# Last 128 output rows projected by column halves, and batch 1's second half of head pairs moved up, in a fused attention and feed-forward kernel

## Chip, cores and metric

The kernel runs on one core of a Trainium2 chip. The metric is the device time of one execution in microseconds, as the median over several executions. All times below come from the profiled execution or from those runs.

## The reference

For each of 8 batches and 8 heads, with 576 tokens of width 64, attention without a softmax is computed, normalised and scaled per head; the heads are then joined to rows of width 512, and a feed-forward layer of width 2048 follows.

```python
kv  = einsum('bhsd,bhse->bhde', k, v)
o   = einsum('bhsd,bhde->bhse', q, kv)
rms = sqrt(mean(o * o, axis=-1, keepdims=True) + 1e-06)
x   = (o / rms * g_norm).transpose(0, 2, 1, 3).reshape(4608, 512)
h   = x @ w_in                                # 4608 x 2048
out = (h / (1 + exp(-1.702 * h))) @ w_out     # 4608 x 512, float32
```

## The kernel before

The 4608 rows are cut into nine tiles of 512 rows. Tiles 0 to 7 each hold 512 of the 576 tokens of one batch. The remaining 64 tokens of each of the eight batches together make tile 8, called t == B in the code; its input is x_rem.

The function dense works on one tile in two phases. In the first phase TensorE makes 16 blocks of the hidden layer, four accumulating matmuls each (hidden, line 439), and ScalarE applies the gate to each block (line 448) and writes gT. In the second phase the function project (lines 478 to 506) multiplies gT by w_out: for each of four row blocks mo of 128 rows, 16 matmuls of 512 columns (fo, line 482) accumulate into one PSUM bank. The bank is copied to osb in SBUF, and DMAs store the rows. For tiles 0 to 7 one copy by VectorE (or by ScalarE for odd mo in tile 0, which is called deep) moves the whole bank. For tile 8 VectorE copies columns 0 to 255 (line 492), then ScalarE columns 256 to 511 (line 493), and two DMAs, one on SyncE's queue (SP) and one on ScalarE's, each store 64 rows of 512 columns (line 506).

The attention of tile t + 1 is woven into tile t by hand. The two dictionaries units1 and units2 hold small steps: a step under key n of units2 is issued right after the n-th projection matmul. Every engine executes its own instructions strictly in the order in which they are written, so this order decides what waits behind what. In tile 0 the projection is interleaved: 16 groups of four matmuls, going round mo = 0, 1, 2, 3 four times. The bank of mo = 0 is therefore complete after step 51, that of mo = 1 after step 55, that of mo = 2 after step 59 and that of mo = 3 after step 63.

During tile 0's second phase, batch 1 is prepared by the class Second, for four head pairs c = 0 to 3:

- pack_k(c) (line 95) is a VectorE copy that rearranges keys from kraw into kbuf.
- kv(c) (line 408) is six matmuls on kbuf and vbuf. After an odd c, keep_kv (line 228) copies the two products on VectorE into kvb, as two instructions.
- out(c) (line 247) is one 512-column matmul that needs kvb, and then a Square on ScalarE (line 267).
- ss(c) is a matmul that sums the squares (line 325), and then Ln (line 327) and Exp (line 333) on ScalarE.
- apply(c) (line 339) is one VectorE instruction that multiplies the attention output by the scale and writes xT, the input of tile 1.

The steps of pairs 0 and 1 and of pairs 2 and 3 are placed in this way before the change: pack_k after steps 21, 21, 36, 36; kv after 23, 24, 43, 44; out after 27, 33, 47, 52; ss and apply seven steps after each out.

PSUM has eight banks in three pools: ps_a with three (tag "att": attention products), ps_h with three (hidden blocks, the banks of mo = 0 and 1 in tile 0, and batch 1's sums of squares) and ps_o with two (projection outputs, among them mo = 2 and 3 in tile 0). A new tile in a pool waits until the earlier user of its bank is done.

Tile 1 begins with four hidden blocks worked side by side (group = 4, called hG), in the order of ko and then of block. Blocks 0 to 2 take banks of ps_h, and the fourth takes one of ps_o (line 452). From block 4 on, the hidden blocks (hT) take a ps_h bank each in turn.

Of the kernel before, what the change touches and what calls it, by code (L numbers as in the profile page):

```python
# [8 lines left out]
F32 = mybir.dt.float32  # L9
# [3 lines left out]
P = 128  # L13
# [3 lines left out]
def kernel(  # L17
# [10 lines left out]
    nc = tc.nc  # L28

    B, H, S, D = q.shape  # L30
    DM = H * D
    DFF = moe_w_in.shape[1]
    NPAIR = H // 2
    FO = DFF // P
    KO = DM // P
    EPS = 1e-6
    SM = 512
    J = SM // P
    R = S - SM
    assert R == 64 and B * R == SM and KO == NPAIR and 2 * D == P  # L40
    NT = B + 1
    EARLY = 2
    PE_ = 96
    NJ = S // PE_
# [8 lines left out]
    ps_a = ctx.enter_context(tc.tile_pool(name="ps_a", bufs=3, space=bass.MemoryType.PSUM))  # L53
    ps_h = ctx.enter_context(tc.tile_pool(name="ps_h", bufs=3, space=bass.MemoryType.PSUM))
    ps_o = ctx.enter_context(tc.tile_pool(name="ps_o", bufs=2, space=bass.MemoryType.PSUM))
# [22 lines left out]
    w_out_sb = const.tile([P, FO, DM], F16)  # L78
# [66 lines left out]
    for n, queue in (("k", nc.sync), ("q", nc.scalar), ("v", nc.sync)):  # L145
# [3 lines left out]
            out=first[n].rearrange("p (h x) -> p h x", h=2), in_=early_src(n, 0, 0, 1)  # L149
# [7 lines left out]
        out=ident,  # L157
        in_=ident,
# [35 lines left out]
    class Attention:  # L194
        ss_pool = (ps_a, "att")

        def __init__(self, b):
            self.b, self.kb = b, kvb[b % 2]
            self.qT, self.o = {}, {}
            x = xpool.tile([P, KO * SM], F16, name="xT", tag="xT")  # L200
            if b < EARLY:
                self.x = xT[b] = x.rearrange("p (c n) -> p c n", c=KO)
# [231 lines left out]
    def dense(t, units1, units2, group, deep):  # L434
        x = xT.pop(t) if t < B else x_rem
        gT = gpool.tile([P, FO, SM], F16, name="gT", tag="gT")

        def hidden(h, fo, ko):
            nc.tensor.matmul(  # L439
                h,  # L440
                w_in_sb[:, ko, fo * P : (fo + 1) * P],
                x[:, ko],
                start=(ko == 0),
                stop=(ko == KO - 1),
            )

        def gate(h, fo):
            nc.scalar.activation(gT[:, fo, :], h, AFT.Gelu_apprx_sigmoid)  # L448

        hs = []  # L450
        for i in range(group):
            pool, tag = (ps_h, "hT") if i < 3 else (ps_o, "o") if i < 5 else (ps_a, "att")
            hs.append(pool.tile([P, SM], F32, name="hG", tag=tag))
        if group:
            if t == 0:
                order = [(ko, fo) for f in (0, 2) for ko in (0, 1) for fo in (f, f + 1)]
                order += [(2, fo) for fo in range(4)]
                order += [(ko, fo) for ko in (0, 1, 2) for fo in (4, 5)]
                order += [(KO - 1, fo) for fo in range(group)]
            else:  # L460
                order = [(ko, fo) for ko in range(KO) for fo in range(group)]
            for ko, fo in order:
                hidden(hs[fo], fo, ko)
            for fo in range(group):
                gate(hs[fo], fo)
        for fo in range(FO):
            if fo >= group:
                h = ps_h.tile([P, SM], F32, name="hT", tag="hT")
                for ko in range(KO):
                    hidden(h, fo, ko)  # L470
                gate(h, fo)
            for u in units1.get(fo, ()):
                u()

        osb = opool.tile([P, 4, DM], F32, name="osb", tag="osb")
        os = {}

        def project(mo, fo):
            if fo == 0:
                pool, tag = (ps_h, "hT") if deep and mo < 2 else (ps_o, "o")  # L480
                os[mo] = pool.tile([P, DM], F32, name="o", tag=tag)
            nc.tensor.matmul(  # L482
                os[mo],
                gT[:, fo, mo * P : (mo + 1) * P],
                w_out_sb[:, fo, :],
                start=(fo == 0),
                stop=(fo == FO - 1),
            )
            if fo == FO - 1:
                if t == B:  # L490
                    half = DM // 2
                    nc.vector.tensor_copy(osb[:, mo, 0:half], os[mo][:, 0:half])  # L492
                    nc.scalar.copy(osb[:, mo, half:DM], os[mo][:, half:DM])
                else:
                    copy = nc.scalar.copy if deep and mo % 2 else nc.vector.tensor_copy
                    copy(osb[:, mo, :], os[mo])  # L496
                if t == B:
                    for g in range(2):
                        rows = out[(2 * mo + g) * S : (2 * mo + g + 1) * S, :]
                        if 2 * mo + g < EARLY:  # L500
                            p0 = SM % PE_
                            rows = rows[bass.DynSlice(NJ * p0 + SM // PE_, R, step=NJ), :]
                        else:
                            rows = rows[SM:S, :]
                        queue = (nc.sync, nc.scalar)[g]
                        queue.dma_start(out=rows, in_=osb[g * R : (g + 1) * R, mo, :])

        if deep:
            steps = [(mo, 4 * i + k) for i in range(4) for mo in range(4) for k in range(4)]
        else:  # L510
            steps = [(mo, fo) for mo in range(4) for fo in range(FO)]
        for n, (mo, fo) in enumerate(steps):
            project(mo, fo)
            for u in units2.get(n, ()):
                u()
        if t < EARLY:

            n = 0
            while n < SM:
                mo, j, p = n // P, n // PE_, n % PE_  # L520
                m = min((mo + 1) * P, (j + 1) * PE_) - n
                nc.sync.dma_start(
                    out=out[t * S : (t + 1) * S, :][bass.DynSlice(NJ * p + j, m, step=NJ), :],
                    in_=osb[n % P : n % P + m, mo, :],
                )
                n += m
        elif t < B:
            nc.sync.dma_start(
                out=out[t * S : t * S + SM, :].rearrange("(p j) m -> p j m", j=J), in_=osb
            )  # L530
# [76 lines left out]

    for t in range(NT):
        b = t + 1
        u1, u2 = {}, {}  # L610

        def at1(i, f, *args):
            u1.setdefault(i, []).append(lambda: f(*args))

        def at2(i, f, *args):
            u2.setdefault(i, []).append(lambda: f(*args))

        def of(b, name, *args):
            return lambda: getattr(live[b], name)(*args)

        if t == 0:
            at1(7, of(0, "out", NPAIR))
            at2(4, setattr, a0, "ss_pool", Attention.ss_pool)
            at2(4, of(0, "ss", NPAIR, True))
            at2(4, of(0, "apply", NPAIR))
            at1(8, start, 1)
            at1(9, spread_g)
            for r in krem + vrem:
                at1(8, nc.vector.memset, r[R:P], 0.0)
            for c in range(NPAIR):  # L630
                at1(12, of(1, "pack_q", c))
                at2(9 + 3 * c, of(1, "q", c))
                at2((21, 21, 36, 36)[c], of(1, "pack_k", c))
                at2((23, 24, 43, 44)[c], of(1, "kv", c))
                o = (27, 33, 47, 52)[c]
                at2(o, of(1, "out", c))
                at2(o + 7, of(1, "ss", c))
                at2(o + 7, of(1, "apply", c))
            at2(14, load_batch, 2, vbuf[0:1, NPAIR - 1, 0:1])
        elif b < B:  # L640
            if t == 1:
                at2(46, setattr, live[1], "ss_pool", Attention.ss_pool)
                at2(46, of(1, "out", NPAIR))
                at2(53, of(1, "ss", NPAIR))
                at2(53, of(1, "apply", NPAIR))
            f0 = 7 if t == 1 else 2
            at1(f0, casts, b)
            at1(f0, start, b)
            at1(f0, of(b, "transpose_q"))
            if t + 2 < B:  # L650
                at1(f0, load_batch, t + 2)
            for c in range(NPAIR):
                at1((11 if t == 1 else 9) + c, of(b, "kv", c))
            at2(0, nc.scalar.preload_act_table_set, "natural_log_exp_and_others")
            for j in range(J):
                at2((1, 4, 8, 11)[j], of(b, "rows", j))
            at2(7, of(b, "turn", 0))
            at2(16, of(b, "turn", 2))
            at2(27, of(b, "out", NPAIR))
            at2(36, of(b, "ss", NPAIR))  # L660
            at2(36, of(b, "apply", NPAIR))
        dense(t, u1, u2, (6, 4)[t] if t < 2 else 0, t == 0)


# [28 lines left out]
```

## Time and profile before

| | us |
|---|---|
| median of 9 runs | 290.96 |
| lowest and highest run | 290.54, 291.59 |
| the profiled execution, its own time | 291.17 |
| span of the profiled execution | 289.4 |
| TensorE busy in the span | 280.6 |
| ScalarE busy | 151.1 |
| VectorE busy | 102.8 |
| GpSimd busy | 56.4 |

The span runs from the first to the last instruction in the trace; the execution's own time has 1.77 us around it. An engine's busy time is the union of the durations of its instructions. A matmul's listed duration includes its way through the array, so successive matmuls overlap in the list; what a matmul costs in a stream is the distance between two starts. The chain of waits goes back from the last instruction to whatever released each step. The word "issue" in it is time in which nothing that the trace shows was waited for.

### The profile page before, as it was taken

What the parts mean: (1) busy time and instruction counts of PE and PEld (TensorE: products, weight loads), DVE (VectorE), ACT (ScalarE), POOL (GpSimd) and SP (SyncE); (2) the same over time, 40 slices, a digit from 0 to 9 for tenths busy, and PEclk for the clock granted to TensorE, in tenths of its full rate; (3) what the DMA queues carried; (4) which work ended last, traced back from release to release, by engine and by line L of the source; (5) the groups of instructions that cost most, each with busy time, mean ns of one, the idle gap of its engine ahead of it and who ended that gap; (6) DMA issues with size and microseconds to landing.
All of it is one profiled execution on the core that took longest, in us unless ns stands there. A gap on an engine that the chain in (4) does not pass through costs nothing.

```text
span 289.4 us, 4052 instructions
## 1 busy us (share of the span) xinstructions
PE 280.6 (97%) x1598; PEld 134.8 (47%) x1598; DVE 102.8 (36%) x222; ACT 151.1 (52%) x263; POOL 56.4 (19%) x71
## 2 busy tenths in 40 slices
PE   7989999999999999999999999999999999999993
PEld 2434544455445544554455445544454444444441
DVE  2530434545461456037602760275218200110010
ACT  2667546856465644574457536653664364027310
POOL 8841000203500170008000710062005100000000
PEclk9999999999999999999999999999999999999998
DMA  8999999979989736892699658944601320020022
GB/s 175 198 207 205 204 176 349 215 179 352 194 192 323 168 73 188 259 269 54 181 200 333 69 163 218 338 72 127 138 0 23 86 111 0 0 112 35 0 73 73
DMA packets 67636, 45.79 MB, mean 158 GB/s; under 512 B 37666, under 2 KB 65314, under 8 KB 66850
## 3 DMA queue, kind: packets, MB, share of 16 engines
q1 hardware_dynamic: 58080, 37.43, 50.3%
q0 software_dynamic: 9008, 7.29, 16.0%
q10 hardware_dynamic: 530, 0.82, 1.0%
q8 instruction: 12, 0.20, 0.3%
q14 instruction: 6, 0.05, 0.1%
HBM read 36.70 MB, written 9.44 MB: 159 GB/s over the span
## 4 chain that ended last, share of the span: by engine, by line
PE 91%; DMA 3%; POOL 3%; ACT 1%; DVE 1%; issue 0%; POOLq 0%
PE o L482 42%; PE hT L439 40%; PE hG L439 3%; DMA w_in_sb<-in_moe_w_in_dram 3%; PE kvp L213 2%; PE outR L279 2%; POOL vbuf L88 1%; POOL qraw L88 1%; POOL kraw L88 1%; PE kvp L408 1%; PE kvp L221 0%; PE ss L325 0%; PE outT L247 0%; PE q L421 0%; PE outT L258 0%
## 5 line engine op out<-in xcount | busy, mean ns | idle before, releaser
L482 PE MATMUL o<-w_out_sb,gT 128*128 128x512 f16 x576 | 134.0, 379 | 0.0
L448 ACT ACTIVATE gT<-hT 128x512 f16<-128x512 f32 x134 | 80.0, 599 | 76.5 <-PE hT L439 76.5
L439 PE MATMUL hT<-xT,w_in_sb 128*128 128x512 f16 x472 | 107.4, 379 | 0.0
L439 PEld LDWEIGHTS <-w_in_sb 128*128 128x128 f16 x576 | 55.1, 98 | 63.5 <-issue 1.3
L482 PEld LDWEIGHTS <-gT 128*128 128x128 f16 x576 | 54.6, 98 | 57.9
L309 POOL TENSOR_TENSOR x<-xr,g_all 128x512 f16<-128x512 f32 x24 | 30.0, 1270 | 129.9 <-DVE xr L304 84.6
L496 DVE COPY osb<-o 128x512 f32<-128x512 f32 x30 | 20.6, 687 | 46.5 <-PE o L482 46.5
L290 DVE TENSOR_REDUCE sum<-sq 128x8 f32<-128x512 f16 x24 | 15.3, 678 | 23.9 <-ACT sq L287 23.9
L228 DVE CAST kvb<-kvp 64x256 f16<-64x256 f32 (+1 forms) x16 | 6.2, 389 | 43.1 <-PE kvp L221 42.0
L304 DVE TENSOR_TENSOR xr<-outR,sum 128x512 f32<-128x512 f32 x24 | 15.5, 686 | 4.9 <-ACT sum L301 4.0
L267 ACT ACTIVATE sq<-outT 128x512 f16<-128x512 f32 (+1 forms) x16 | 7.8, 488 | 13.0 <-PE outT L247 11.6
L327 ACT ACTIVATE ln<-ss,eps_t 128x512 f32<-128x512 f32 (+1 forms) x16 | 9.3, 580 | 9.6 <-PE ss L325 9.4
L439 PE MATMUL hT<-x_rem,w_in_sb 128*128 128x512 f16 x64 | 14.0, 379 | 0.0
L287 ACT ACTIVATE sq<-outR 128x512 f16<-128x512 f32 x24 | 12.9, 589 | 0.1
L300 ACT ACTIVATE sum<-sum,eps_t 128x16 f32<-128x16 f32 x12 | 3.7, 308 | 14.8 <-DVE sum L290 14.8
L136 DVE CAST qbuf<-qf 128x512 f16<-128x512 f32 x24 | 9.7, 468 | 3.6 <-DMA qf<-in_q_dram 3.6
L492 DVE COPY osb<-o 128x256 f32<-128x256 f32 x4 | 1.7, 425 | 25.7 <-PE o L482 25.7
L448 ACT ACT_TABLE_LOAD x8 | 10.3, 1283 | 0.1
L279 PEld LDWEIGHTS <-qTd 128*128 128x128 f16 x96 | 7.4, 98 | 5.7 <-issue 0.2
L213 PEld LDWEIGHTS <-kbuf 128*128 128x128 f16 x96 | 7.4, 98 | 5.7
L439 PE MATMUL hG<-xT,w_in_sb 128*128 128x512 f16 x40 | 9.3, 379 | 0.5 <-DMA w_in_sb<-in_moe_w_in_dram 0.5
L213 PE MATMUL kvp<-vbuf,kbuf 128*128 128x128 f16 x96 | 9.3, 219 | 0.0
(70 smaller groups left out, 150.6 us busy)
## 6 DMA issues: line engine op xcount, KB each, us to landing
kf<-in_k_dram SPq DMA_DIRECT2D x6, 1024.0 KB, 5.9
vf<-in_v_dram SPq DMA_DIRECT2D x6, 1024.0 KB, 8.4
qf<-in_q_dram SPq DMA_DIRECT2D x6, 1024.0 KB, 11.9
out_dram<-osb SPq DMA_DIRECT2D x6, 1024.0 KB, 4.2
w_out_sb<-in_moe_w_out_dram POOLq DMA_DIRECT2D x4, 512.0 KB, 17.2
out_dram<-osb SPq DMA_DIRECT2D x6, 192.0 KB, 2.6
out_dram<-osb SPq DMA_DIRECT2D x8, 128.0 KB, 2.4
w_in_sb<-in_moe_w_in_dram POOLq DMA_DIRECT2D x3, 256.0 KB, 8.0
```

The lines of the kernel that those rows point to most:

```text
L136: nc.vector.tensor_copy(out=dst[:, c, :, :].rearrange("p j (l d) -> p j l d", l=2), in_=src[n][:, h, :].rearrange("p l (j d) -> p j l d", ...
L213: nc.tensor.matmul(t[:, c, :].rearrange("p (l d) -> p l d", l=2), kh[:, c, j, :], vh[:, 2 * c : 2 * c + 2, j * D : (j + 1) * D], start=(j ...
L279: nc.tensor.matmul(t[:, c * P : (c + 1) * P], self.qT[c][:, j * P : (j + 1) * P], self.kb[:, c, :], start=True, stop=True,)
L287: nc.scalar.activation(sq, t, AFT.Square)
L290: nc.vector.tensor_reduce(out=self.sum2[:, j % 2, :], in_=sq.rearrange("p (h d) -> p h d", h=H), op=ALU.add, axis=mybir.AxisListType.X,)
L304: nc.vector.tensor_mul(xr, self.o[j + i].rearrange("p (h d) -> p h d", h=H), s2[:, i, :].unsqueeze(2).to_broadcast([P, H, D]),)
L309: nc.gpsimd.tensor_mul(self.x16[:, j + i, :].rearrange("p (h d) -> p h d", h=H), xr, g_all.unsqueeze(1).to_broadcast([P, H, D]),)
L327: nc.scalar.activation(ln[:, 0:n], t[:, 0:n], AFT.Ln, bias=eps_t, scale=1.0 / D)
L439: nc.tensor.matmul(h, w_in_sb[:, ko, fo * P : (fo + 1) * P], x[:, ko], start=(ko == 0), stop=(ko == KO - 1),)
L448: nc.scalar.activation(gT[:, fo, :], h, AFT.Gelu_apprx_sigmoid)
L482: nc.tensor.matmul(os[mo], gT[:, fo, mo * P : (mo + 1) * P], w_out_sb[:, fo, :], start=(fo == 0), stop=(fo == FO - 1),)
L496: copy(osb[:, mo, :], os[mo])
```

## The change

The change has three parts.

- In tile 8, the last row block (mo = 3) is taken out of project and goes through a new function, project_last. It runs 16 matmuls of 256 columns for columns 0 to 255 into one ps_a bank, copies them by ScalarE and stores them with two DMAs; then 16 matmuls for columns 256 to 511 into another ps_a bank, a copy by VectorE and two DMAs. The row blocks 0, 1 and 2 of tile 8 are copied whole by one engine each (VectorE, ScalarE, VectorE) where two engines copied half of each.
- In tile 0, pack_k of pairs 2 and 3 moves from step 36 to 33, kv from 43 and 44 to 42 and 43, out of pair 1 from 33 to 31 and of pair 2 from 47 to 48, and ss and apply from 34, 40, 54, 59 to 34, 38, 54, 58.
- In tile 1 the fourth hG block takes a ps_a bank where it took a ps_o bank.

```diff
+    LAST = ((0, DM // 2), (DM // 2, DM))
...
-            pool, tag = (ps_h, "hT") if i < 3 else (ps_o, "o") if i < 5 else (ps_a, "att")
+            pool, tag = (ps_h, "hT") if i < 3 else (ps_o, "o") if i < 5 and t == 0 else (ps_a, "att")
...
             if fo == FO - 1:
+                copy = nc.scalar.copy if (deep or t == B) and mo % 2 else nc.vector.tensor_copy
+                copy(osb[:, mo, :], os[mo])
                 if t == B:
-                    half = DM // 2
-                    nc.vector.tensor_copy(osb[:, mo, 0:half], os[mo][:, 0:half])
-                    nc.scalar.copy(osb[:, mo, half:DM], os[mo][:, half:DM])
+                    store_rest(mo, 0, DM)
+
+        def store_rest(mo, n0, n1):
+            for g in range(2):
+                rows = out[(2 * mo + g) * S : (2 * mo + g + 1) * S, n0:n1]
...
+                queue = (nc.sync, nc.scalar)[g]
+                queue.dma_start(out=rows, in_=osb[g * R : (g + 1) * R, mo, n0:n1])
+
+        def project_last(mo):
+            for i, (n0, n1) in enumerate(LAST):
+                o = ps_a.tile([P, n1 - n0], F32, name="oh", tag="att")
+                for fo in range(FO):
+                    nc.tensor.matmul(
+                        o,
+                        gT[:, fo, mo * P : (mo + 1) * P],
+                        w_out_sb[:, fo, n0:n1],
+                        start=(fo == 0),
+                        stop=(fo == FO - 1),
+                    )
+                copy = nc.vector.tensor_copy if i else nc.scalar.copy
+                copy(osb[:, mo, n0:n1], o)
+                store_rest(mo, n0, n1)
...
-            steps = [(mo, fo) for mo in range(4) for fo in range(FO)]
+            steps = [(mo, fo) for mo in range(4 - (t == B)) for fo in range(FO)]
...
+        if t == B:
+            project_last(3)
...
-                at2((21, 21, 36, 36)[c], of(1, "pack_k", c))
-                at2((23, 24, 43, 44)[c], of(1, "kv", c))
-                o = (27, 33, 47, 52)[c]
+                at2((21, 21, 33, 33)[c], of(1, "pack_k", c))
+                at2((23, 24, 42, 43)[c], of(1, "kv", c))
+                o = (27, 31, 48, 52)[c]
                 at2(o, of(1, "out", c))
-                at2(o + 7, of(1, "ss", c))
-                at2(o + 7, of(1, "apply", c))
+                at2(o + 7 - c // 2, of(1, "ss", c))
+                at2(o + 7 - c // 2, of(1, "apply", c))
```

More of the change, by code (lines that the diff above doesn't have):

```diff
@@ L489, in project @@
             if fo == FO - 1:
+                copy = nc.scalar.copy if (deep or t == B) and mo % 2 else nc.vector.tensor_copy
+                copy(osb[:, mo, :], os[mo])
                 if t == B:
-                    half = DM // 2
-                    nc.vector.tensor_copy(osb[:, mo, 0:half], os[mo][:, 0:half])
-                    nc.scalar.copy(osb[:, mo, half:DM], os[mo][:, half:DM])
-                else:
[L495 to L506, printed above, removed]
+                    store_rest(mo, 0, DM)
+        def store_rest(mo, n0, n1):
+            for g in range(2):
+                rows = out[(2 * mo + g) * S : (2 * mo + g + 1) * S, n0:n1]
+                if 2 * mo + g < EARLY:
+                    p0 = SM % PE_
+                    rows = rows[bass.DynSlice(NJ * p0 + SM // PE_, R, step=NJ), :]
+                else:
+                    rows = rows[SM:S, :]
+                queue = (nc.sync, nc.scalar)[g]
[14 more added lines that the diff above has]
+                store_rest(mo, n0, n1)
         if deep:
```

## The prediction

> **What bounds the kernel now.** I read the page's busy line first, then its chain of waits, then that chain piece by piece where TensorE leaves it, then the timelines of single engines there.
>
> ```profile
> PE 280.6 (97%) x1598; PEld 134.8 (47%) x1598; DVE 102.8 (36%) x222; ACT 151.1 (52%) x263; POOL 56.4 (19%) x71
> PE 91%; DMA 3%; POOL 3%; ACT 1%; DVE 1%; issue 0%; POOLq 0%
> ```
>
> TensorE is 97% busy and holds 91% of the chain. A kernel like this gains only where TensorE stands still or after its last matmul. From 16.8 us on, the chain leaves TensorE for more than a few hundredths in just one place of the middle. This is that stretch of the chain (start, length, what):
>
> ```profile
> 40.37 0.46 ACT sq L267
> ...
> 41.58 0.64 ACT rs L333
> 42.22 0.03 issue
> 42.24 0.75 DVE xT L339
> 42.99 0.27 DVE kbuf L95
> 43.27 0.05 issue
> 43.31 0.51 PE kvp L408 x6
> 43.82 0.22 PE o L482
> 44.04 0.34 PE kvp L408 x6
> 44.38 0.65 PE o L482 x3
> 45.03 0.03 issue
> 45.06 0.39 PE outT L247
> ```
>
> kv(2) at 43.31 waits for pack_k(2), which stands on VectorE behind apply(0), which waits for the Exp of pair 0. The loss is read from starts: 512-column matmuls start every 0.2158 us (64 in 13.81 us), steps 41 to 43 start at 42.12, 42.34 and 42.55, so kv(2) could start at 42.77. It starts 0.54 later. In the same way out(2) could start at 44.86 and starts at 45.06, 0.20 late, because it waits for keep_kv. VectorE's timeline shows why keep_kv is late: apply(1) is ahead of it.
>
> ```profile
> 43.70 0.75 DVE L339 SCALAR_TENSOR_TENSOR xT<-outT,g_col,rs 128x512 f16<-128x512 f32 x1 [0.18 <-ACT rs L333]
> 44.41 0.59 DVE L228 CAST kvb<-kvp 64x128 f16<-64x128 f32 x2
> ```
>
> The weight loads at the start of tile 1 show the third place:
>
> ```profile
> 49.17 0.53 PEld L439 LDWEIGHTS <-w_in_sb 128*128 128x128 f16 x3
> 49.90 0.10 PEld L439 LDWEIGHTS <-w_in_sb 128*128 128x128 f16 x1 [0.19 <-issue]
> 50.22 0.31 PEld L439 LDWEIGHTS <-w_in_sb 128*128 128x128 f16 x2 [0.22 <-issue]
> ```
>
> A load starts with the matmul before it, so hG2 started at 49.90, not 49.82, and hG3 at 50.22, not 50.12. hG2 waits for the Ln of pair 3 (ends 49.84), hG3 for VectorE's copy of mo = 2 (ends 50.16).
>
> The end, on the timeline:
>
> ```profile
> 284.62 0.42 DVE L492 COPY osb<-o 128x256 f32<-128x256 f32 x1 [3.03 <-PE o L482]
> 285.07 0.37 ACT L493 COPY osb<-o 128x256 f32<-128x256 f32 x1 [3.08 <-DVE osb L492]
> 285.47 0.47 SPq L506 DMA_DIRECT2D out_dram<-osb  x1
> 285.48 0.50 ACTq L506 DMA_DIRECT2D out_dram<-osb  x1
> ```
>
> The half copies do not run side by side: ScalarE waits for VectorE, and only then the stores go out. Windows of 0.2 us show their data moving from about 286.5 to 287.65; the span ends at 289.4.
>
> **What the Trainium skill says.** "PSUM — Partial Sum Buffer", section "PSUM bank collisions raise a hardware error", has two engines on one bank kept apart even for disjoint columns; the trace agrees (285.07 after 285.04). "TensorE: Matmul & The Clock Gate", "Back-to-back issue gap", gives N/2.4 + 2.5 ns per matmul of N columns: 215.8 and 109.2 ns for 512 and 256. The trace has 215.8, and 0.11 us for the 256-column ss. "DMA: Bandwidth & Descriptors", "Anatomy of one DMA", says that about 2 us of a DMA are fixed. The stores agree: 64, 128 and 192 KB land in 2.3, 2.4 and 2.6 us.
>
> **The end, part by part.** TensorE: 16 matmuls of 512 become 32 of 256. In place of 16 x 215.8 ns stand 32 x 109.2 ns: +0.04 us. Does the doubled number of weight loads bind? A load's row says 98 ns, but six kv pairs of load and 128-column matmul take 0.34 us in the chain, 57 ns a pair, so loads overlap; a pair of 109 ns leaves room. Bounds: +0.04, and +3.1 if nothing overlapped (32 x (98 + 109) ns against 3.45 us). I take +0.04.
>
> After the last matmul: one VectorE copy of 128x256 (0.42, the row above), then the stores. ScalarE's 0.37 with its two handovers, 285.04 to 285.48, leaves the path: -0.44, less about 0.04 for the handover that VectorE's copy then makes to the stores: -0.40.
>
> The stores: two of 64 KB in place of two of 128 KB. Their data took 1.15 us. If time follows bytes, half goes, -0.55; if it follows landing of a single store (2.4 to 2.3), -0.10. Packets are 1 KB in place of 2 KB, as many as before, so not all of the half can go. I take -0.25.
>
> The first half's work is covered: its matmuls end 1.75 us before the last one, ScalarE copies in 0.37, the two stores are issued for 0.5 on SP and ScalarE, and both queues are free 0.8 us before the last matmul ends. Its data, going by the old delay of 1.0 us from issue, moves in the 0.8 us before VectorE's last copy finishes. Without that cover it would delay the last stores by at most its own data time, 0.6. The whole-bank copies of mo = 0, 1, 2 take 0.69 on VectorE (or 0.57 on ScalarE) where the halves took 0.82; 3.45 us of matmuls hide them. The ps_a banks have been idle since tile 7's attention. Sum of the end: 0.04 - 0.40 - 0.25 = -0.61; bounds -0.46 and -0.91.
>
> **The middle, step by step.** No DMA is moved in tile 0, and nothing on SP or GpSimd is passed. Moved are VectorE's two packs (0.35 each, 0.61 as a pair) ahead of apply(0), and TensorE's and ScalarE's steps by a few matmuls. The packs need kraw: its DMA was issued at 20.90 and such loads took 18.3 to 18.7, so it lands at about 39.5; VectorE is free from 38.38. They end by 40.3, with apply(0) due at 42.2.
>
> Up to out(0) at 38.44 nothing changes. Then: steps 28 to 31 to 39.52, out(1) 39.52, its Square 39.93; steps 32 to 34, ss(0) at 40.39 as before. Ln(0) follows its end at 40.81 (0.06 sooner, the Square is out of the way), Exp(0) 0.71 later at 41.52, apply(0) 0.66 later at 42.18. Ln(1) can start 0.54 after Exp(0) (the gap from 48.15 to 48.69 between Exp and the next ScalarE instruction): 42.06, with ss(1) done at 41.84. Exp(1) 42.78, apply(1) 43.44, keep_kv 0.71 later at 44.15, and out(2) 0.65 after that (45.06 - 44.41): 44.80.
>
> TensorE meanwhile: after ss(1) steps 39 to 42 end at 42.54, kv(2) starts without a wait, step 43, kv(3), steps 44 to 48 end at 44.52. So out(2) waits 0.28: the wait at kv(2) goes, and keep_kv behind apply(1) is late next. Before, out(2) at 45.06 had one step less behind it, so the gain is 45.06 + 0.22 - 44.80 = 0.48. Bounds: 0.74 if VectorE did not hold it, and 0.32 if kv(2) gets the bank of out(0) and waits for apply(0).
>
> From out(3) on, the distances on all engines stay as they were (ss(3) is one step sooner but its Ln waits for ScalarE, as now). hG2 keeps its 0.08. hG3's 0.10 must go: apply(3) now stands before mo = 2's copy on VectorE, which would end near 51.5 instead of 50.16, but the ps_a bank that comes round, that of kv(2) and kv(3), is free since 44.8. Had hG3 stayed in ps_o it would cost almost 2 us. hT4 waits for the first gate as now. hT4, at 53.22 before, starts at 52.64: -0.58.
>
> Does tile 1 keep it? Its kv of batch 2 starts at 60.12 and needs VectorE's cast of vbuf, which a DMA sets (the query block lands at 54.9; casts of q, k and the first v end at 59.14). It would start at 59.54: the cover of 1.0 shrinks to 0.4. The transposed queries land at 62.6, first used at 65.1, later 64.5. Later tiles load a tile ahead. So all of it arrives.
>
> **Sum.** -0.58 - 0.61 = -1.2. The profiled execution, 291.17, would become 290.0 with a span of 288.2. It lies 0.21 above the median; the median 290.96 becomes 289.8.
>
> **Rivals.** (1) The middle is taken back: the last matmul comes only as much sooner as the end gives, since batch 2's casts or keep_kv's wait behind apply(1) take the place of the old waits. For it: the 0.4 us of cover and the VectorE queue; against it: the casts' DMAs do not move. Time 290.96 - 0.61 = 290.35. (2) The stores are nearly all latency, so the end gives only 0.36 + 0.10: 290.96 - 0.58 - 0.46 = 289.9, near the forecast; with the kv(2) bank wait as well, 290.2. (3) Slower: the 32 short pairs at the end are bound by weight loads. Fully serial they add 3.1, giving 290.96 - 1.2 + 3.1 = 292.9; it outweighs the gain from 109 + 1200/32 = 147 ns a pair on. Against it: the 57 ns above. For it: no stream of more than a dozen short pairs is in the trace. (4) No change: both gains shrink to their lower ends and the loads shift; 290.7.
>
> **How the numbers follow.** Forecast 0.54, rival (1) 0.20, (2) 0.12, (3) 0.06, (4) 0.08. A measurement of this kernel tells 0.2%, 0.58 us, from no change, so 290.38 is the border. The forecast, (2) and half of (1) are faster: 0.76; the other half of (1) and (4) are within it: 0.18; (3) is slower: 0.06. The low end takes the bounds together, 0.84 in the middle and 0.91 at the end: 289.2. The high end, 290.6, includes rival (1) with the runs' scatter and leaves out (3) and (4).
>
> **What would show it.** Right: no wait before kv(2) at 42.5, out(2) at about 44.8 behind keep_kv, hG3 without its gap, hT4 near 52.6; at the end 32 matmuls in 3.5 us, one VectorE copy ahead of the last stores, and about 4.2 us from the last matmul to the end of the span, against 4.8. Wrong: pairs over 0.12 us, an idle TensorE before tile 1's kv, or stores that land no sooner after their issue.

## The result: 0.39% less, and the profile after

| | before | after |
|---|---|---|
| median, us | 291.06 (54 runs) | 290.0 (17 runs) |
| lowest and highest | 290.32, 292.3 | 288.82, 290.9 |
| profiled execution, its own time | 291.17 | 289.82 |
| its span | 289.4 | 288.0 |

The ratio is 0.9961, 95% interval 0.9951 to 0.9972: faster by 0.28 to 0.49%. The time lies 0.2 us from the forecast of 289.8 and inside its range. The total came out, but not by the forecast's sum, as the profile after shows. (The ratios leave out single executions that took over 1.5% longer than the fastest of the same kernel.)

The page of the changed kernel, its busy line and the two lines of its chain of waits:

```profile
PE 281.3 (98%) x1614; PEld 136.6 (47%) x1614; DVE 102.9 (36%) x221; ACT 150.5 (52%) x261; POOL 56.5 (20%) x71
PE 71%; DMA 19%; POOL 3%; SPq 3%; DVE 2%; issue 1%; POOLq 0%; DVEq 0%
PE hT L440 34%; PE o L483 32%; DMA vbuf<-in_v_dram 6%; DMA qf<-in_q_dram 5%; DMA w_in_sb<-in_moe_w_in_dram 5%; DMA vrf<-in_v_dram 2%; PE kvp L214 2%; PE outR L280 2%; DMA xT<-x 2%; PE oh L512 1%; SPq L115 1%; SPq L120 1%; POOL w_in_sb L181 1%; POOL qraw L89 1%; POOL vbuf L89 1%
```

TensorE stands at 98%, but its share of the chain has fallen from 91% to 71%, and DMAs hold 19% where they held 3%. The chain no longer follows TensorE back to the first loads of weights. It leaves TensorE where tile 2 begins. This is that piece of it, start, length and what:

```profile
68.20 6.84 DMA vrf<-in_v_dram
75.03 4.38 DMA xT<-x
79.42 0.05 issue
79.46 1.68 PE hT L440 x7
```

And TensorE's own timeline there:

```profile
76.67 0.27 PE L326 MATMUL ss<-sq,ones 128*128 128x256 f16 x1
76.78 2.32 PE L483 MATMUL o<-w_out_sb,gT 128*128 128x512 f16 x10
79.46 1.04 PE L440 MATMUL hT<-xT,w_in_sb 128*128 128x512 f16 x4 [0.36 <-DMA xT<-x]
```

The last ten matmuls of tile 1 start 0.2158 us apart from 76.78, so tile 2 could begin at 78.94. It begins at 79.46, 0.52 us late (the 0.36 in brackets counts from the modelled end of the last matmul). It waits for the DMA transposes of batch 2's x, the input of tile 2, to land (the moment at which the profile shows a transfer as complete). Before, tile 1's last ten began at 77.69 and tile 2 at 79.85, without a wait.

The middle itself went as worked out. VectorE, and then TensorE at the same place:

```profile
43.17 0.75 DVE L340 SCALAR_TENSOR_TENSOR xT<-outT,g_col,rs 128x512 f16<-128x512 f32 x1 [0.49 <-ACT rs L334]
43.84 0.58 DVE L229 CAST kvb<-kvp 64x128 f16<-64x128 f32 x2
```

```profile
42.36 0.50 PE L409 MATMUL kvp<-vbuf,kbuf 96*128 96x128 f16 x6
...
44.47 0.39 PE L248 MATMUL outT<-qT,kvb 128*128 128x512 f16 x1
...
48.58 3.69 PE L440 MATMUL hG<-xT,w_in_sb 128*128 128x512 f16 x16
...
52.31 1.89 PE L440 MATMUL hT<-xT,w_in_sb 128*128 128x512 f16 x8
```

kv(2) starts without a wait, out(2) waits for keep_kv behind apply(1), and the hG group is 0.10 us shorter (3.69 against 3.79). The first hT starts at 52.31 against 53.22. Of these 0.91 us, 0.26 were there before the first moved step (out(0) at 38.18 against 38.44), so the moved steps gave 0.65. The 0.26 are scatter and no part of the change: over the profiles of all the kernels below, out(0) starts between 37.67 and 38.58.

The end, on the timeline and in windows of 0.2 us (columns: busy of PE, PEld, DVE, ACT, POOL, then clock, DMA share and GB/s):

```profile
284.28 0.42 DVE L520 COPY osb<-oh 128x256 f32<-128x256 f32 x1 [2.80 <-PE oh L512]
284.73 0.47 SPq L505 DMA_DIRECT2D out_dram<-osb  x1
284.74 0.50 ACTq L505 DMA_DIRECT2D out_dram<-osb  x1
```

```profile
285.80:286.00 0.20, 0.00 (x0) 0.00 (x0) 0.00 (x0) 0.00 (x0) 0.00 (x0) 1.00 0.53 133
286.00:286.20 0.20, 0.00 (x0) 0.00 (x0) 0.00 (x0) 0.00 (x0) 0.00 (x0) 1.00 0.82 190
286.20:286.40 0.20, 0.00 (x0) 0.00 (x0) 0.00 (x0) 0.00 (x0) 0.00 (x0) 1.00 1.00 256
286.40:286.60 0.20, 0.00 (x0) 0.00 (x0) 0.00 (x0) 0.00 (x0) 0.00 (x0) 1.00 0.35 77
```

The same windows before, the first with much data and the last two with any:

```profile
286.60:286.80 0.20, 0.00 (x0) 0.00 (x0) 0.00 (x0) 0.00 (x0) 0.00 (x0) 1.00 1.11 256
...
287.40:287.60 0.20, 0.00 (x0) 0.00 (x0) 0.00 (x0) 0.00 (x0) 0.00 (x0) 0.50 0.93 358
287.60:287.80 0.20, 0.00 (x0) 0.00 (x0) 0.00 (x0) 0.00 (x0) 0.00 (x0) 0.50 0.14 41
```

The spans end at 289.38 before and at 288.04 now. From the start of VectorE's last copy to the end of the span it is 3.76 us, against 4.76 before: 1.00 us less, where the forecast had 0.65 for this stretch. The copy and its handovers give 0.40, from 284.62 to 285.47 before, from 284.28 to 284.73 now. The rest, 0.60, comes after the stores are issued. Read from the single packets in the trace, the last stores' data move from 286.60 to 287.75 before, 1.15 us, and from 285.86 to 286.58 now, 0.72 us. That is 0.43 of the 0.60; the other 0.17 lie between the last data and the end of the span (1.63 against 1.46).

So the 1.34 us between the two profiled spans are: 0.26 from an earlier start, 0.65 from the moved steps, -0.52 from the wait at tile 2, -0.05 from the 32 short matmuls, and 1.00 at the end. Theory A is the forecast's sum. Theory B says that the end is worth about 1.0 us, and that x of batch 2, held up by batch 3's loads, which SP issues ahead of it, takes back most of the middle.

### The profile page after: what moved, and what is told of

It is laid out like the page before. It is cut to its first block, busy times and chain, and to the rows that moved or that the text cites. A ratio compares the mean times of both kernels' runs of the same rounds, so it can differ in the third digit from the quotient of the medians.

```text
span 288.0 us, 4085 instructions
## 1 busy us (share of the span) xinstructions
PE 281.3 (98%) x1614; PEld 136.6 (47%) x1614; DVE 102.9 (36%) x221; ACT 150.5 (52%) x261; POOL 56.5 (20%) x71
## 4 chain that ended last, share of the span: by engine, by line
PE 71%; DMA 19%; POOL 3%; SPq 3%; DVE 2%; issue 1%; POOLq 0%; DVEq 0%
PE hT L440 34%; PE o L483 32%; DMA vbuf<-in_v_dram 6%; DMA qf<-in_q_dram 5%; DMA w_in_sb<-in_moe_w_in_dram 5%; DMA vrf<-in_v_dram 2%; PE kvp L214 2%; PE outR L280 2%; DMA xT<-x 2%; PE oh L512 1%; SPq L115 1%; SPq L120 1%; POOL w_in_sb L181 1%; POOL qraw L89 1%; POOL vbuf L89 1%
## 5 line engine op out<-in xcount | busy, mean ns | idle before, releaser
L483 PE MATMUL o<-w_out_sb,gT 128*128 128x512 f16 x560 | 130.6, 379 | 0.0
L483 PEld LDWEIGHTS <-gT 128*128 128x128 f16 x560 | 53.0, 98 | 56.1 <-issue 0.2
L492 DVE COPY osb<-o 128x512 f32<-128x512 f32 x32 | 22.0, 688 | 69.0 <-PE o L483 69.0
L561 PE MATMUL idle<-kvb 128*128 128x512 f16 x24 | 8.6, 483 | 1.3 <-DVE kvb L155 1.3
```

The costliest lines, as they stand in the source:

```text
L483: nc.tensor.matmul(os[mo], gT[:, fo, mo * P : (mo + 1) * P], w_out_sb[:, fo, :], start=(fo == 0), stop=(fo == FO - 1),)
```

## The experiments

All were timed beside the kernel before, and all ratios are to it; what is said of a difference from the changed kernel goes through these ratios. A tenth of a per cent is 0.29 us.

**One part alone: the end.** The steps and the pool choice of the kernel before are put back.

```diff
-                at2((21, 21, 33, 33)[c], of(1, "pack_k", c))
-                at2((23, 24, 42, 43)[c], of(1, "kv", c))
-                o = (27, 31, 48, 52)[c]
+                at2((21, 21, 36, 36)[c], of(1, "pack_k", c))
+                at2((23, 24, 43, 44)[c], of(1, "kv", c))
+                o = (27, 33, 47, 52)[c]
...
-            pool, tag = (ps_h, "hT") if i < 3 else (ps_o, "o") if i < 5 and t == 0 else (ps_a, "att")
+            pool, tag = (ps_h, "hT") if i < 3 else (ps_o, "o") if i < 5 else (ps_a, "att")
```

> Only the end of the change: the last row block by column halves, schedule and PSUM pools as before. Theory A (the sum as forecast): 0.61 us less than before, ratio 0.9979. Theory B (read from the trace of the changed kernel: from the last matmul to the end of the span 4.82 us became 3.76 us): about 1.0 us less, ratio 0.9965, and that distance again 3.7 to 3.9 us.

Measured: 289.78 us, ratio 0.9959 (0.9946 to 0.9972). In its profile the last copy starts at 284.02 and the span ends at 287.79, 3.77 us. The end alone is as fast as the whole change, within the intervals.

**One part alone: the middle.** The kernel before with the moved steps and the ps_a bank, the same lines of the diff the other way.

> Only the moved steps of batch 1 and the fourth hG block in ps_a; the end as before. Theory A: 0.58 us less than before, ratio 0.9980, TensorE without a wait where tile 2 begins. Theory B (tile 2's first block waits for the transposed x of batch 2, which batch 3's loads hold up and which lands near 79.3 us whatever TensorE does): TensorE waits 0.3 to 0.6 us there, and only 0 to 0.35 us arrives at the end, ratio 0.999 to 1.0.

Measured: 290.89 us, ratio 0.9991 (0.9979 to 1.0003). What TensorE waits for in this kernel, longest first (total, times, longest):

```profile
...
PE hG L439 <- DMA w_in_sb<-in_moe_w_in_dram: 0.4, 1, 0.4
PE hT L439 <- DMA xT<-x: 0.3, 1, 0.3
...
PE kvp L213 <- DVE vbuf L134: 0.2, 1, 0.2
```

The second line is the wait at tile 2, and the third one is tile 1's kv of batch 2 waiting for the cast of vbuf: the cover that the forecast saw shrink to 0.4 us is used up in this execution. A gain of 0.65 us in the middle leaves 0.26; the interval goes from a gain of 0.6 to a loss of 0.1.

**The pool choice undone.**

```diff
-            pool, tag = (ps_h, "hT") if i < 3 else (ps_o, "o") if i < 5 and t == 0 else (ps_a, "att")
+            pool, tag = (ps_h, "hT") if i < 3 else (ps_o, "o") if i < 5 else (ps_a, "att")
```

> The changed kernel with the fourth hG block back in ps_o. It should wait for VectorE's copy of mo = 2, which now stands behind apply(3): about 1.8 us of idle TensorE at the start of tile 1. Theory A: all of it arrives, 1.8 us more than the changed kernel, 0.8 more than before (ratio 1.003). Theory B: the wait at tile 2's start (0.36 us) goes and pays for a part: 1.4 us more than the changed kernel, ratio 1.001, and no wait for x at tile 2.

Measured: 290.37 us, ratio 0.9977 (0.997 to 0.9985), 0.5 us more than the changed kernel, though the two intervals still overlap slightly. Both sizes were wrong, for hG3 waited for another copy:

```profile
48.79 0.88 PE L440 MATMUL hG<-xT,w_in_sb 128*128 128x512 f16 x3
50.42 2.97 PE L440 MATMUL hG<-xT,w_in_sb 128*128 128x512 f16 x13 [0.76 <-ACT osb L492]
```

It took the bank of mo = 3, which ScalarE had copied by 50.38, not that of mo = 2, copied by VectorE from 50.60 to 51.28. hG2 is in its place, 0.08 late as ever, so hG3 was due at 49.52 and came 0.90 late. Tile 2 begins at 80.06, without a wait. Of 0.90 us added to TensorE, 0.5 show in the time, and the wait of 0.52 in the changed kernel, which is gone here, makes up about the difference.

**The last stores as large as before.**

```diff
                 copy(osb[:, mo, n0:n1], o)
-                store_rest(mo, n0, n1)
+            store_rest(mo, 0, DM)
```

> The changed kernel, but the two halves of the last row block are stored together after the second copy, as two DMAs of 128 KB. This takes back the smaller last stores alone. Theory A: 0.25 us more than the changed kernel, ratio to before 0.997. Theory B: 0.35 (data time 1.03 against 0.67 us) to 0.65 us more (if the shorter rest after the data belongs to the small stores too), ratio 0.9975 to 0.9985.

Measured: 290.98 us, ratio 0.9993 (0.9981 to 1.0004), 0.9 us more than the changed kernel. The intervals of the two ratios allow 0.26 to 1.5. In its profile, from the last copy at 284.21 to the end at 288.58, it is 4.37 us, 0.61 more than in the changed kernel. The windows of its stores:

```profile
285.80:286.00 0.20, 0.00 (x0) 0.00 (x0) 0.00 (x0) 0.00 (x0) 0.00 (x0) 1.00 0.84 205
...
286.60:286.80 0.20, 0.00 (x0) 0.00 (x0) 0.00 (x0) 0.00 (x0) 0.00 (x0) 1.00 1.08 420
286.80:287.00 0.20, 0.00 (x0) 0.00 (x0) 0.00 (x0) 0.00 (x0) 0.00 (x0) 1.00 0.25 82
```

Issued at 284.70, the stores move data from 285.82 to 286.98 by the trace's packets, 1.16 us, as before and 0.44 more than in the changed kernel (the expectation's 1.03 and 0.67 are too short by the packets). This part is the store size. Between the last data and the end of the span it is 1.60 us here, 0.14 more than in the changed kernel. That part does not follow the size: it is 1.34 us with the same large stores in two profiles further down (the small loads by GpSimd, in the middle alone and in the kernel before), and 1.71 with the small stores in two others (the same loads by GpSimd in the changed kernel, at once and held back). What sets it no run shows.

**Two matmuls more.** The changed kernel with 0.43 us of unused matmuls after block 9 of tile 1.

```diff
+            def extra():
+                x = ps_a.tile([P, SM], F32, name="extra", tag="att")
+                for _ in range(2):
+                    nc.tensor.matmul(x, w_in_sb[:, 0, 0:P], w_in_sb[:, 0, 0:SM], start=True, stop=True)
+
+            if t == 1:
+                at1(9, extra)
```

> The changed kernel with two more 512-column matmuls in the middle of tile 1's first phase, 0.43 us of TensorE, whose result nobody uses. Theory A (TensorE sets the pace everywhere): 0.43 us more than the changed kernel, ratio to before 0.9976. Theory B (x of batch 2 sets when tile 2 begins): tile 2 begins where it did, near 79.4 us, its wait shrinks by what was added, 0 to 0.2 us more, ratio 0.9961 to 0.9968.

Measured: 290.02 us, ratio 0.9959 (0.9946 to 0.9971): they cost nothing that can be measured, though the two intervals leave room for up to 0.6 us, so the time by itself doesn't exclude 0.43. The profile says more. The DMA transposes of x in this kernel (duration of issue, first and last start; then time to landing):

```profile
L315 SPq DMA_TRANSPOSE xT<-x x2: 1867/2236/2606, 72.3 to 75.2; - x2
...
DMA to landing us min/median/max: 4.0/5.1/6.1
```

The second one, issued at 75.2, lands 4.0 us later at 79.2. Tile 1's last ten matmuls, which begin at 77.08, are done just then, and tile 2 begins at 79.25, as early as x allows.

**The same two matmuls in the kernel before**, as a control.

> The control: the kernel before with the same two matmuls. It had no wait for x at tile 2, so by both theories all 0.43 us show, ratio 1.0015, and tile 2 begins 0.43 us later, at about 80.3 us, without a wait.

Measured: 291.41 us, ratio 1.0004 (0.9998 to 1.0011). The profile is as expected: tile 2 begins at 80.22, without a wait. The time is not: 0.1 us shows, at most 0.3, of the 0.43. In the timed runs of the kernel before, part of an addition is absorbed too, so the times of this pair do not tell the two kernels apart. In its profile x landed at 80.01, only 0.2 us before tile 2 began. Whether TensorE waits for x in some of the other executions isn't seen, since only one has a trace.

**No loads of batch 3.** Left out are all loads of batch 3; tile 3 and batch 3's part of tile 8 are computed from batch 2's inputs.

```diff
-            if t + 2 < B:
+            if t == 1:
+                at1(f0, lambda: staged.update({3: staged[2]}))
+            elif t + 2 < B:
                 at1(f0, load_batch, t + 2)
```

> The changed kernel without any load of batch 3: tile 3 is computed from the staged inputs of batch 2 (the 512 and the 64 tokens both), so its output rows are batch 2's. Left out is what stands ahead of the transposes of batch 2's x on SP's queue. If those loads set when x arrives (theory B): the transposes land in about 3 us, in place of 4.4 and 6.2, x is there by 78.2 us, TensorE's 0.2 to 0.5 us at tile 2's start goes in every run, and the kernel takes 0.2 to 0.5 us less than the changed one (ratio to before 0.9945 to 0.9955). If x is late for a reason before batch 3's loads: the wait stays and the ratio is 0.996.

Measured: 289.32 us, ratio 0.9944 (0.993 to 0.9957). The transposes in this kernel:

```profile
L315 SPq DMA_TRANSPOSE xT<-x x2: 1233/1236/1240, 71.4 to 74.6; - x2
...
DMA to landing us min/median/max: 3.1/3.6/4.2
```

The last lands at 77.6 and TensorE doesn't wait. The kernel is 0.5 us faster than the changed one, as theory B had it. The two intervals overlap a little, so the size is loose, but the wait and its cause are shown: batch 3's loads hold up batch 2's x.

They hold up its landing more than its issue. x is made by GpSimd out of tile 1's attention products, and the second transpose goes out once GpSimd is done. GpSimd's last piece of it, before and in the changed kernel:

```profile
73.25 2.50 POOL L309 TENSOR_TENSOR x<-xr,g_all 128x512 f16<-128x512 f32 x2 [0.65 <-DVE xr L304]
72.34 2.50 POOL L310 TENSOR_TENSOR x<-xr,g_all 128x512 f16<-128x512 f32 x2 [0.64 <-DVE xr L305]
```

It ends at 75.75 before and at 74.84 in the changed kernel. The second transpose went out at 75.78 and at 75.03, and landed at 79.32 and at 79.42: sent 0.75 us sooner, it landed no sooner. Without batch 3's loads it went out at 74.56 and took 3.1 us; in the ten profiles in which loads of batch 3 were still under way then, it took 3.4 to 4.4. Whether it stands behind them in a queue or shares the DMA engines with them isn't told apart.

Across the profiled executions in which batch 3's loads stand on SP's queue and TensorE was late, tile 2 began a nearly constant time after the first of those loads was issued: 62.51 to 79.46 in the changed kernel, 62.64 to 79.64 with the middle alone, 62.33 to 79.39 with large stores, 62.11 to 79.09 with an uneven cut, all 17.0 us (61.99 to 79.20, 17.2 us, with the end alone, where the wait was 0.1). In the profile before, x landed 17.2 us after the first of the loads, at 79.32, and tile 2 began at 79.85: 0.5 us of slack, into which the middle's gain fell. (In the changed kernel's profile these loads also went out 0.39 us later than before, so the size of the wait differs from one execution to another.)

**Three attempts to move the small loads.** krf, vrf and qrf of batch 3 keep SP issuing for 7 us ahead of the transposes. GpSimd was given them, in the changed kernel, in the middle alone and in the kernel before; load_batch passes its new last argument on to these loads.

```diff
-                at1(f0, load_batch, t + 2)
+                at1(f0, load_batch, t + 2, None, nc.gpsimd if t == 1 else nc.sync)
```

> The changed kernel, with batch 3's loads of the last 64 tokens (krf, vrf, qrf: four DMAs that keep SP issuing for 7 us ahead of the transposes of batch 2's x) issued by GpSimd, idle at that time. If those loads hold up x (theory B): x lands before 78.9 us, TensorE's 0.5 us at tile 2's start goes, 0.4 to 0.5 us less than the changed kernel, ratio to before about 0.9945. Theory A (all of the middle arrives already): no change, 0.9961. Theory C (the three 1 MB loads ahead of x hold it up, not these): the wait stays at 0.3 us or more.

> The end as before; the moved steps, the ps_a bank and batch 3's loads of the last 64 tokens by GpSimd. Theory B: the wait at tile 2's start is gone and the whole of the middle arrives, 0.5 to 0.65 us less than before, ratio 0.998, against 0.9991 without the GpSimd loads. Theory A: the same 0.998 as the middle alone ought to have had. Theory C: 0.999 as the middle alone.

> The control: the kernel before with batch 3's loads of the last 64 tokens by GpSimd and nothing else. Theory B: nothing, since TensorE didn't wait at tile 2's start before (ratio 1.0, at most 0.1% either way). If these loads are a cost of their own, independent of the change: 0.4 us less, 0.9985.

Measured: 0.9998 (0.9978 to 1.0019), 1.0013 (0.9997 to 1.0029) and 1.0032 (1.0013 to 1.0051); single runs went from 289.52 to 298.24 us, and the medians of all executions are 291.98, 292.2 and 292.12, against 291.05 before. None of the theories had this. The profiled executions took 295.42, 296.24 and 298.15 us, well over these medians. In the first of the three, the transpose of batch 2's queries is the one that comes late:

```profile
L233 SPq DMA_TRANSPOSE qTd<-qbuf x1: 3425/3425/3425, 58.1 to 58.1; - x1
...
  PE outR L280: 4.0, 1
...
DMA to landing us min/median/max: 10.2/10.2/10.2
```

It landed 10.2 us after its issue, against 4.7 before, and TensorE waited 4.0 us. GpSimd had issued the loads at 57.22 to 60.4, beside it. In the other two profiles it landed after 10.7 and 11.4 us. The times say nothing on the wait at tile 2. But when x's second transpose went out, late, at 78.64, the last of batch 3's loads had landed (77.27), and it took 3.1 us, as without these loads. And there was little to gain from SP's issuing: in the changed kernel SP was done with the small loads at 72.3, before GpSimd had all of x.

**The same loads, held back until the queries are there.**

```diff
+            if rest is nc.gpsimd and n == "k":
+                nc.gpsimd.tensor_copy(t[0:1, 0, 0:1], live[b - 1].qTr[0:1, 0, 0:1])
```

> The changed kernel with batch 3's loads of the last 64 tokens issued by GpSimd, held back until batch 2's queries are transposed (a one-element GpSimd copy reads them first), so that they don't delay that transpose. Theory B: x of batch 2 lands before TensorE asks for it near 78.9 us, the 0.2 to 0.5 us wait at tile 2's start goes, 0.2 to 0.5 us less than the changed kernel, ratio to before 0.9945 to 0.9955. Theory C (the three 1 MB loads hold x up): the wait stays, 0.996. Theory A: no change, 0.996.

Measured: 290.77 us, ratio 0.9991 (0.9983 to 1.0), slower than the changed kernel. Its profiled execution has no wait at tile 2 (79.01, span 287.9), but its own time, 289.67, is the lowest of 13. What the others lost can't be seen. In this profile the small loads had landed by 72.5 and the large ones by 77.2; in the changed kernel the large ones had by 74.6 and the small ones by 77.9. x came at 78.97 and 79.42, so it was late whichever of them came last, and which of them holds it up stays open.

**An uneven cut.** The last row block in 384 and 128 columns.

```diff
-    LAST = ((0, DM // 2), (DM // 2, DM))
+    LAST = ((0, 3 * DM // 4), (3 * DM // 4, DM))
```

> The changed kernel with the last row block cut into 384 and 128 columns. VectorE's last copy falls from 0.42 to about 0.29 us and the last stores from 64 to 32 KB each. If the end is set by that copy and by the data of the last stores: 0.2 to 0.3 us less than the changed kernel from the last matmul to the end of the span (3.5 us in place of 3.76). If the stores of the first 384 columns, now issued only about 0.5 us ahead of the last, collide with them: no gain.

Measured: 289.81 us, ratio 0.9952 (0.9936 to 0.9968). The last copy takes 0.29 us as estimated. From it to the end of the span it is 3.58 us, 0.18 less than in the changed kernel, of which the copy is 0.13. So the smaller last stores bring little. The first part's stores still move data until about 285.4, while the last ones are issued at 284.23; that this is the reason isn't shown. By the times this kernel isn't told apart from the changed one.

## Why the prediction came true, and where it was wrong

- **Removal of the wait at kv(2), keep_kv late next, hG3's bank.** Right. The moved steps gave 0.65 against 0.58: out(2) came 0.07 earlier than the sum had it, as keep_kv followed apply(1) by 0.67 and not 0.71, and out(2) that by 0.63 and not 0.65. The "almost 2 us" for hG3 left in ps_o were 0.90, as it took the other bank.
- **"Later tiles load a tile ahead. So all of it arrives."** Wrong; this step failed. The check stopped at tile 1's kv and its queries and took the later tiles as covered. Tile 2's input isn't a load but the transposes of x, which tile 1 itself sends through SP's queue behind batch 3's loads. It landed at 79.32 before and at 79.42 after, though GpSimd had it ready 0.9 us sooner. Of 0.65 us, 0.13 passed in the profile; the middle alone measured 0.26, interval from a gain of 0.6 to a loss of 0.1. The answer stood in the profile before: the second transpose was issued at 75.78 and landed 3.54 us later, 0.5 before tile 2 began. This is rival (1)'s outcome by a wait that it did not name.
- **The copy off the path.** Right: 0.40 forecast, 0.40 measured.
- **The short matmuls.** Right: 32 pairs took 3.51 us, 110 ns each. Rival (3), pairs bound by weight loads, is out. The section of the Trainium skill that the forecast names, "TensorE: Matmul & The Clock Gate", "Back-to-back issue gap", gives the formula for a single matmul, and 131 ns at 512 columns for a stream of weight loads and matmuls; the 215.8 ns of the stream in this trace decide. Fully serial pairs would have cost 3.2 us, not 3.1.
- **"I take -0.25" for the stores.** Mis-sized: -0.60 in the profile. The data time fell by 0.43, from 1.15 to 0.72 us, inside the bounds of -0.10 and -0.55; the other 0.17 came after the data, in a stretch that differs by more than that between profiles with equal stores. The smaller bound came from median landings by size, 2.4 and 2.3 us; of this last pair, SP's store landed in 2.32 us before and in 1.94 now. The Trainium skill, "DMA: Bandwidth & Descriptors", "Anatomy of one DMA", gives its fixed 2 us for transfers that GpSimd issues; these are issued by SP and ScalarE, so the landings in the trace decide. Rival (2), stores that are nearly all latency, is out: the end gave 1.0 us and not 0.46.
- **The cover of the first half's work.** Right: its stores were issued at 282.93, and their data ended at 284.79, 1.07 us before the last stores' data began.

The first error took 0.52 us from the sum, the second added 0.35 and the moved steps 0.07 more than forecast, so the total fell near the forecast by luck. The end alone carries the measured gain. The middle adds 0.3 us alone and nothing beside the end, by the ratios; the intervals allow up to 0.6.

## What to carry to other kernels

When time is taken out of the busiest engine early in a kernel, follow the gain to every later place where that engine reads something from a DMA, and read each landing against the present start; the smallest slack caps what arrives (here 0.5 us). Where loads are issued ahead of a transfer, do not assume that it lands sooner because it is sent sooner: here x was sent 0.75 us sooner and landed 0.1 later. At the end of this kernel the size of the last stores counted as much as the copy before them (0.43 us of data time against 0.40), so it is worth reading the data time of the last pair of stores together.

## What the runs showed of the hardware that was not expected

- In three profiled executions, of 295.42 to 298.15 us, loads of 64-token rows issued by GpSimd ran beside a DMA transpose on SP's queue, and that transpose landed in 10.2 to 11.4 us, in place of 4.7. With these loads held back it landed in 4.9.
- Two last stores of 64 KB in place of 128 KB moved their data in 0.72 us in place of 1.15, which is more than half.
- A transpose of x sent while other loads were under way landed in 3.4 to 4.4 us, against 3.1 without them.
- The fourth hG block took whichever of the two ps_o banks came free first in the trace: that of mo = 2 before (50.16 us), that of mo = 3 with the pool choice undone (50.38 against 51.28). Whether this is settled when the program is built isn't shown.
